# Zeros of the expert table written during attention, input sums by DMA, and a changed order of boxes, casts and router steps

## The chip, the cores and the metric

The kernel runs on one core of a Trainium2 chip. The metric is the device time of one execution in microseconds (us). Engines: PE (TensorE, matmuls), DVE (VectorE), ACT (ScalarE), POOL (GpSimd) and SP (SyncE, which here only issues DMAs). Each engine runs its own instructions in the order in which the program issues them, and waits on semaphores for the others. DMAs are issued on the queues of SP, ACT and POOL.

## The reference

Three stages follow each other.

```python
# attention: B=4, H=8, S=576, D=64; heads 0-3 local (32), heads 4-7 strided (32)
scores = np.where(masks, scale * q @ k.T, -1e9); attn = softmax(scores); x = attn @ v
x = transpose(x).reshape(2304, 512)
# gated unit: d_ff = 1536
x = ((1 / (1 + np.exp(-(x @ w_gate)))) * (x @ w_val)) @ w_out
# routed experts: E = 8, F = 1024; only tokens with x @ w_skip > 0
e_idx = argmax(x @ w_gate2); gate_w = softmax(x @ w_gate2)[e_idx]
out = x;  out[do_compute] += gate_w * (relu(x @ w1[e]) @ w2[e])
```

Everything is float32.

## The kernel before

**Numbers.** Products in float32 are made of three matmuls (`mm3`, L592): each operand is split into a high part, cast to `fp32r` by ACT, and a low part, operand minus high, made by DVE. `xh`, `xl` are parts of the inputs, `wh`, `wl` of the weights.

**Attention (0 to 119 us).** 32 steps, each one batch and a pair of heads. A string of letters (`ORDERS` and its default, L874) says in which order a step issues its pieces: scores on PE, row maxima on DVE, exponentials on ACT, the reciprocal of sums on DVE (L308), the norm on POOL (L314), the transposing "flip" on PE (L323), the product with V on PE (L339), and from there a copy into `xf`, the transposed input of the next stage (L345, L351). `a`, `D` and `p` in the string take one job from the background queues of ACT, DVE and POOL. Three more steps drain the pipeline and hold pieces of the first block (`G`). `step_loads` (L819) adds DMAs and background jobs at fixed steps.

**Blocks (to about 396 us).** The tokens are cut into six units of 384, in three pairs p. A pair's products with a pair of weight chunks f are done by a scheme of seven products: the inputs B11, B21, B22 and sums T1 to T4 of the four quarters (`SUMS`: T1 = B12 − B11, T3 = B22 − B12, T2 = B22 − T1, T4 = B21 − T2), the weights A11, A12, A22 and sums S1 to S4. `combine` (L411) makes a job for a T, `operand` (L421) the jobs for its high and low. `stage_sums` (L517) makes the S, `split_w` (L526) the highs (L534) and lows (L537) of a weight block. `period` (L673) issues one block (f, p) interleaved with the end of the block before it: products (`mm`, L593 to L595), copies from PSUM on ACT (L625, L632, L636) and sums on DVE (L639, L655, L658, L666), then stores by DMA (L644). Its `freed` mark lets the next block's highs take the buffers. Weight bits are converted on DVE (L460, L464, L469, L489). "Boxes" `wof` hold two chunks of the out-weights and their sums (`out_weights`, L550), which are stored by DMA. `raws_left` is the list of raw weights in the order in which they are fetched.

**Stage 2 (396 to 552 us).** The product with w_out, 63 steps (`NSTEP`). `at(k, ...)` hangs extra work on a step. `load_x` and `load_w` fetch the stored sums; `turn_back` (L1073) multiplies with the identity and the router weights at once, and reads the result as rows (L1088, ACT) and router sums (L1089, DVE). `pick` chooses the expert, `place` (L1130) computes slots and scatters the rows by indirect DMA (L1147) to the table `xs` in DRAM. `init_xs` (L1189) writes zeros into the table before that, 13 DMAs on SP at steps 9 to 15.

**Experts.** For each of eight experts: fetch rows of `xs`, transpose (`prep`), hidden rows (`hidden`, L1478: matmuls L1488, sums L1501, the operation `h` L1508), outputs (`output_steps`, L1565). `split_e` (L1165) splits the expert's weights, high on ACT (L1168), low on DVE or POOL (L1169). The last unit's router (unit 5) is run inside expert 0's first rows, at the end of the function.

The lines on which the low parts and the sums rest:

```python
nc.vector.tensor_tensor(xl[p, nm][:, part, :], source(p, nm)[:, part, :], h.bitcast(F32), op=ALU.subtract)   # L433
e.tensor_tensor(source(p, nm)[:, part, :], x, y, op=ALU.subtract)                                           # L417
eng = nc.gpsimd if e and (i % 2 if e == 1 else i < 4) else nc.vector                                        # split_e
```

Of the kernel before, what the change touches and what calls it, by code (L numbers as in the profile page):

```python
# [14 lines left out]
I32 = mybir.dt.int32  # L15
# [8 lines left out]
def kernel(  # L24
# [73 lines left out]
    xs = dram.tile([NE * SLOTS, TW], F32, name="xs")  # L98
    vcm = dram.tile([B, S, 4 * D], F32, name="vcm")
# [231 lines left out]

    def apply_v(it, s, pT):
# [77 lines left out]

    def combine(p, nm, eng, parts, cost):  # L411

        e = nc.gpsimd if eng == "P" else nc.vector
# [7 lines left out]
    def operand(p, nm, parts, hc, lc):  # L421

        for part in parts:
            def high(part=part):
# [4 lines left out]
                nc.scalar.copy(xh[p, nm][:, part, :], source(p, nm)[:, part, :])  # L429

            def low(part=part):
                h = xh[p, nm][:, part, :]
                nc.vector.tensor_tensor(  # L433
                    xl[p, nm][:, part, :], source(p, nm)[:, part, :], h.bitcast(F32), op=ALU.subtract)

            j = Job("A", hc, high, [sum_job[p, nm]] if nm[0] == "T" else [])
            x_jobs.setdefault((p, nm), []).append(Job("D", lc, low, [j]))
# [79 lines left out]
    def stage_sums(f):  # L517
        for i, x, y, op in ((4, 0, 1, ALU.add), (5, 4, 2, ALU.subtract), (6, 2, 0, ALU.subtract), (7, 3, 5, ALU.subtract)):
            def fn(i=i, x=x, y=y, op=op):
                nc.vector.tensor_tensor(stage(f, i), stage(f, x), stage(f, y), op=op)  # L520
# [152 lines left out]
    def period(k, prev):  # L673
# [144 lines left out]

    def step_loads(t):  # L819
        clock[0] += 1  # L820
        b, j = divmod(t, 8)
# [53 lines left out]
    for t in range(NS + 3):  # L875
        for c in ORDERS.get(t, "eSfEmIFnaNDTMRpDAaL"):
# [17 lines left out]
    raws_left += [(NC - 1, "o")]  # L894
# [105 lines left out]
    for f, p in BL:  # L1000
# [72 lines left out]
    def turn_back(u, a):  # L1073
# [7 lines left out]
        for m in range(nb):  # L1081
# [83 lines left out]
    def split_e(e, i, raw):  # L1165
        eng = nc.gpsimd if e and (i % 2 if e == 1 else i < 4) else nc.vector
# [20 lines left out]
    zero = []  # L1187

    def init_xs():  # L1189
        zero = late.tile([128, TW], F32, tag="row", bufs=8, name="zero")  # L1190
        nc.gpsimd.memset(zero, 0.0)
        nc.gpsimd.memset(zero[:, TW - 1:TW].bitcast(I32), 1 << 16)
        for i in range(NE * SLOTS // 128):
            nc.sync.dma_start(xs[128 * i:128 * i + 128, :], zero)
            if i % 2:
                yield

# [147 lines left out]
    gx = init_xs()  # L1345
    for k in range(9, 16):
        at(k, gx)
    for p in range(NP):
# [12 lines left out]
        if last:  # L1361
            for k, n in ((15, 1), (16, 2)):
                at(b + k, ta[1], n)
# [446 lines left out]
```

## Time and profile before

| | us |
|---|---|
| median of three runs (lowest, highest) | 745.8 (745.15, 747.28) |
| the profiled execution, own time | 746.98 |
| its span in the profile | 745.3 |
| PE busy | 706.2 |
| DVE busy | 561.6 |
| ACT busy | 452.0 |
| POOL busy | 258.9 |

The mean granted TensorE clock is 0.99 of full speed. The page gives busy time by engine, slices of the span, the chain of waits that ended last, and the costliest groups of instructions. Timelines give for each instruction its start, its duration, the engine and the line, what it writes and reads, and in brackets how long the engine had stood idle before it and what ended that. The waits view sums such idle times by the operation that waited and the one that released it. Windows give the busy time of each engine in a stretch, the granted clock and the share of the DMA engines.

### The profile page before, as it was taken

Reading aid. Unit: us, or ns where it says so; the run is one execution under the profiler, and the core shown is the slowest. Engines: PE = TensorE matmul, PEld = TensorE weight load, DVE = VectorE, ACT = ScalarE, POOL = GpSimd, SP = SyncE. Lnnn points to the kernel's source line nnn. Section 1 sums busy time; section 2 is a strip of 40 time slices with the busy share of each in tenths; the row PEclk is TensorE's granted clock in tenths of the full one; section 3 lists DMA queues with packets and bytes.
Section 4 is the critical chain, followed back from the end, with each engine's and each line's share of the span. In section 5 each row is a group of like instructions: output and inputs, shape, how many; then the busy total and the mean of one; then the engine's idle time right before and its main releaser. Section 6 shows DMA issues by size and latency. Waiting matters only on the chain. (4 is left out here: it accounts for less than half of the span.)

```text
span 745.3 us, 14548 instructions
## 1 busy us (share of the span) xinstructions
PE 706.2 (95%) x4785; PEld 660.1 (89%) x4785; DVE 561.6 (75%) x1246; ACT 452.0 (61%) x1206; POOL 258.9 (35%) x289
## 2 busy tenths in 40 slices
PE   8999988999999999999998989999999999999992
PEld 5766666999999999999888989999988899999991
DVE  3799997989988888888876766677766666666650
ACT  5888986855555555555454855566644766676730
POOL 6577876021040211204033000402324644566611
PEclk9999999999999999999999999999999999999997
DMA  9999610296898888979599996879845687776710
GB/s 199 234 209 220 149 42 30 107 258 187 275 222 256 209 222 228 224 263 202 177 274 335 368 332 180 257 244 303 289 144 186 203 259 246 225 250 223 225 39 14
DMA packets 136857, 158.57 MB, mean 213 GB/s; under 512 B 60510, under 2 KB 105822, under 8 KB 136776
## 3 DMA queue, kind: packets, MB, share of 16 engines
q1 hardware_dynamic: 122072, 134.51, 58.6%
q0 software_dynamic: 11936, 19.66, 12.9%
q10 hardware_dynamic: 2768, 3.41, 1.3%
q8 instruction: 40, 0.66, 0.4%
q14 instruction: 41, 0.34, 0.1%
HBM read 103.49 MB, written 59.65 MB: 219 GB/s over the span
## 5 line engine op out<-in xcount | busy, mean ns | idle before, releaser
L644 POOL DMA_DIRECT2D gT<-sC x36 | 31.9, 1030 | 171.2 <-DVE sC L658 163.9
L301 ACT ACTIVATE sm<-psX,mx 96x128 f32<-96x128 f32 (+2 forms) x176 | 61.8, 375 | 10.1 <-DVE mx L295 7.9
L314 POOL TENSOR_TENSOR sm<-sm,rs 96x384 f32<-96x384 f32 (+2 forms) x64 | 55.5, 885 | 31.6 <-DVE rs L308 18.8
L985 ACT CAST xt<-xt 128x768 fp32r<-128x768 f32 (+1 forms) x74 | 53.9, 742 | 20.5 <-DMA xt<-gB 11.0
L993 DVE TENSOR_TENSOR xt<-xt 128x768 fp32r<-128x768 f32 (+1 forms) x74 | 60.6, 833 | 7.3 <-ACT xt L985 7.2
L639 DVE TENSOR_TENSOR u<-psD,u 128x384 f32<-128x384 f32 x70 | 38.7, 552 | 18.6 <-PE psD L595 18.3
L593 PE MATMUL psD<-xhT,wh 128*128 128x384 f32 x140 | 47.3, 338 | 1.6 <-DVE u L639 1.6
L595 PE MATMUL psA<-xhB,wl 128*128 128x384 f32 x140 | 47.0, 336 | 1.3 <-DVE wl L537 1.3
L595 PE MATMUL psD<-xhT,wl 128*128 128x384 f32 x140 | 47.1, 337 | 0.3 <-DVE wl L537 0.3
L594 PE MATMUL psD<-xlT,wh 128*128 128x384 f32 x140 | 47.0, 336 | 0.0
L594 PE MATMUL psA<-xlB,wh 128*128 128x384 f32 x140 | 46.8, 334 | 0.0
L593 PE MATMUL psA<-xhB,wh 128*128 128x384 f32 x140 | 46.8, 334 | 0.0
L595 PE MATMUL psB<-xhT,wl 128*128 128x384 f32 x140 | 46.8, 334 | 0.0
L593 PE MATMUL psB<-xhT,wh 128*128 128x384 f32 x140 | 46.8, 334 | 0.0
L594 PE MATMUL psB<-xlT,wh 128*128 128x384 f32 x140 | 46.8, 334 | 0.0
L632 ACT COPY psC<-psB 128x384 f32<-128x384 f32 x35 | 16.3, 465 | 43.4 <-PE psB L595 43.4
L1575 POOL DMA_INDIRECT out_dram<-xg x16 | 16.1, 1006 | 73.8 <-DVE xg L1574 65.4
L625 ACT COPY u<-psB 128x384 f32<-128x384 f32 x70 | 33.8, 483 | 11.3 <-PE psB L595 11.1
L1120 POOL COPY row<-lm_all 128x8 f32<-128x8 f32 x18 | 7.9, 478 | 90.1 <-DVE lm_all L1116 90.1
L301 ACT ACTIVATION_READ_ACCUMULATOR sm<-psX,mx 96x1 f32 (+2 forms) x176 | 38.3, 218 | 0.0
L594 PE MATMUL psB<-xt,wtS 128*128 128x384 f32 x108 | 36.3, 336 | 0.9 <-DVE xt L993 0.9
L593 PE MATMUL psB<-xt,wtS 128*128 128x384 f32 x108 | 36.9, 342 | 0.0
(798 smaller groups left out, 2546.7 us busy)
## 6 DMA issues: line engine op xcount, KB each, us to landing
w1r<-in_moe_w_dram SPq DMA_DIRECT2D x28, 512.0 KB
w2r<-in_moe_w_dram SPq DMA_DIRECT2D x28, 512.0 KB
xt<-gT SPq DMA_DIRECT2D x30, 384.0 KB
gT<-u SPq DMA_DIRECT2D x54, 192.0 KB
xt<-gB SPq DMA_DIRECT2D x22, 384.0 KB
gT<-sC POOLq DMA_DIRECT2D x36, 192.0 KB, 6.1
gB<-sA SPq DMA_DIRECT2D x33, 192.0 KB
wg<-in_moe_w_gate_dram SPq DMA_DIRECT2D x12, 512.0 KB
```

What stands on the lines that cost most here:

```text
L301: nc.scalar.activation(sm[:n, w, 0:c], src[:, w, :], AF.Exp, bias=mx[:n, w:w + 1], accum_out=sums[:n, h, w:w + 1])
L314: nc.gpsimd.tensor_tensor(x, x, rs[:n, h, 0:m].rearrange("p (w o) -> p w o", o=1).to_broadcast([n, m, c]), op=ALU.mult)
L593: nc.tensor.matmul(ps, lhsT=whi, rhs=xhi, start=start, stop=False, skip_group_check=skip)
L594: nc.tensor.matmul(ps, lhsT=whi, rhs=xlo, start=False, stop=False, skip_group_check=skip)
L595: nc.tensor.matmul(ps, lhsT=wlo, rhs=xhi, start=False, stop=stop, skip_group_check=skip)
L625: nc.scalar.copy(self.tm[nm], self.ps["B"])
L632: nc.scalar.copy(ps, self.ps[src])
L639: nc.vector.tensor_tensor(self.tm[nm], self.ps["D"], self.tm[nm], op=ALU.add)
L644: nc.gpsimd.dma_start(dst, t, accum_op=ALU.add)
L985: nc.scalar.copy(h.bitcast(F32R), l)
L993: nc.vector.tensor_tensor(l.bitcast(F32R), l, h, op=ALU.subtract)
L1575: ins = nc.gpsimd.indirect_dma_start(out=out[:, :], out_offset=bass.IndirectOffsetOnAxis(ap=xg[t][:n, TW - 1:TW].bitcast(I32), axis=0), in ...
```

## The change

**Zeros.** `init_xs` now runs inside attention. At step 18 three memsets on POOL fill two tiles, two DMAs write them into a DRAM tile `empty` of 128 rows, and at steps 21 to 33 one DMA a step on SP copies it into 128 rows of `xs`.

**Input sums.** Signs are turned so that T1 and the other sums of pair 1, and T1 of pair 2, become additions: `put_x` multiplies by −1 where it copied, and B11's high and low turn it back. A sum is then a copy of one operand by a DMA on SP (`begin_sum`) and a DMA on POOL's queue that adds the other (`accum_op`). The lows of pair 1's B21, T3 and T2 go to POOL. One more background job of POOL is taken in each step after 24.

**Weights and boxes.** `period` asks for block 2's casts and lows (`need(w_jobs[2][0])`) before the sums of the last block of chunk 0. Box 9 is converted before the weights of block 11, and its raw weights are fetched before theirs. The sums S change sign order, with operations of one kind for another.

**Router and tail.** `turn_back` reads the router sums before the rows. Unit 4's and 5's router steps and the transpose of expert 0's rows sit at other steps, unit 5's chain in the tail is written in another order, with the gate's exponential behind it. The odd lows of expert 1 (`split_e`) go from POOL to DVE.

```diff
+    def put_x(dst, src, turned):
+        if turned:
+            nc.vector.tensor_scalar(dst, src, -1.0, None, op0=ALU.mult)
+        else:
+            nc.vector.tensor_copy(dst, src)
...
+    def begin_sum(p, nm):
+        nc.sync.dma_start(source(p, nm), source(p, SUMS[nm][0]))
+
     def combine(p, nm, eng, parts, cost):
...
-                e.tensor_tensor(source(p, nm)[:, part, :], x, y, op=ALU.subtract)
+                t = source(p, nm)[:, part, :]
+                if p == 0 or eng == "D":
+                    (nc.vector if eng == "D" else nc.gpsimd).tensor_tensor(t, x, y, op=ALU.add)
+                else:
+                    nc.gpsimd.dma_start(t, y, accum_op=ALU.add)
...
+                if turned:
+                    nc.vector.scalar_tensor_tensor(l, in0=x, scalar=-1.0, in1=h, op0=ALU.mult, op1=ALU.subtract)
+                else:
+                    (nc.gpsimd if eng == "P" else nc.vector).tensor_tensor(l, x, h, op=ALU.subtract)
...
             if prev.p == NP - 1:
                 freed[prev.f].done = clock[0]
+                if prev.f == 0:
+                    need(w_jobs[2][0])
             prev.store("sC", "u4", 1)
...
+    def init_xs(t):
+        n = NE * SLOTS // RB
+        if t == 18:
+            z, last = temp("zeros"), temp("empty")[:, 0:TW - UT]
+            nc.gpsimd.memset(z, 0.0)
+            nc.gpsimd.memset(last, 0.0)
+            nc.gpsimd.memset(last[:, TW - UT - 1:TW - UT].bitcast(I32), 1 << 16)
+            nc.sync.dma_start(empty[:, 0:UT], z)
+            nc.sync.dma_start(empty[:, UT:TW], last)
+        if 21 <= t < 21 + n:
+            nc.sync.dma_start(xs[RB * (t - 21):RB * (t - 20), :], empty[:, :])
...
-        if t == 22:
-            combine(1, "T1", "P", HALVES, 1.0)
+        if t == 23:
+            begin_sum(1, "T1")
             operand(1, "B11", HALVES, 0.5, 0.5)
-        if t == 26:
+        if t == 25:
+            combine(1, "T1", "P", WHOLE, 0.7)
+        if t == 27:
             for nm in ("T3", "T2", "T4"):
-                combine(1, nm, "P", HALVES, 1.0)
-            for nm in ("B21", "T3", "T2"):
-                operand(1, nm, HALVES, 0.5, 0.5)
-        if t == 30:
-            combine(2, "T1", "P", HALVES, 1.0)
+                begin_sum(1, nm)
+            operand(1, "B21", HALVES, 0.5, 0.9, "P")
+        if t == 29:
+            for nm in ("T3", "T2"):
+                combine(1, nm, "P", WHOLE, 0.7)
+        if t == 31:
+            combine(1, "T4", "P", WHOLE, 0.7)
+            begin_sum(2, "T1")
+        if t == 32:
+            for nm in ("T3", "T2"):
+                operand(1, nm, HALVES, 0.5, 0.9, "P")
+        if t == 33:
+            combine(2, "T1", "P", WHOLE, 0.7)
...
-        for c in ORDERS.get(t, "eSfEmIFnaNDTMRpDAaL"):
+        for c in ORDERS.get(t, "eSfEmIFnaNDTMRpDAaL" + "p" * (t > 24)):
...
-    raws_left += [(NC - 1, "o")]
+    raws_left[-4:] = [raws_left[i] for i in (-2, -4, -3, -1)] + [(NC - 1, "o")]
...
+            if f == NC - 2:
+                out_weights(outs_of[f][0], more_raw)
             if f + 1 < NC:
                 weights(f + 1, more_raw)
-            for i in outs_of[f]:
+            for i in outs_of[f][f == NC - 2:]:
                 out_weights(i, more_raw)
...
-        eng = nc.gpsimd if e and (i % 2 if e == 1 else i < 4) else nc.vector
+        eng = nc.gpsimd if e > 1 and i < 4 else nc.vector
...
-    at(NSTEP - 2, do(lambda: pp.extend(prep(0, head["xg"], PARTS[:1], tag="Y"))))
+    at(NSTEP - 3, do(lambda: pp.extend(prep(0, head["xg"], PARTS[:1], tag="Y", gates=False))))
...
-            for k, n in ((15, 1), (16, 2)):
-                at(b + k, ta[1], n)
+            at(b + 16, ta[1], 3)
...
-            for k in range(18, 21):
-                at(b + k, tb[1])
-            for k in (19, 20):
-                at(b + k, g, 3)
+            at(b + 19, tb[1], 3)
+            at(b + 20, g, 6)
...
-    evict = hidden(1, w, pp, hts, 0, HEAD)
     run(turn_back(NU - 1, 0))
-    evict()
+    evicts = [hidden(1, w, pp, hts, 0, HEAD)]
     run(pick(NU - 1))
-    hide(2, 3)
+    evicts.pop()()
+    evicts = [hidden(2, w, pp, hts, 0, HEAD)]
+    run(place(NU - 1, rank_sums(rst[NU - 1][1])))
+    evicts.pop()()
+    hide(3)
+    gate(xg, pp, 0, HEAD)
     sums = output_steps(0, HEAD, w, hts, xg, pp, settle)
     run(sums, 2)
-    run(place(NU - 1, rank_sums(rst[NU - 1][1])))
```

How the change moves instructions at three places follows. A row is a line of the kernel, an operation, what it writes and reads with a number for each tile, and the shape.

POOL at the end of attention before, from the second half of norm 28 to the last sum (`sm` are the softmax rows, `xT21` is T2 of pair 1, `xT41` its T4, `xT12` T1 of pair 2):

```order
L314 TENSOR_TENSOR sm_2088<-sm_2088,rs_2125 126x2x126
L417 TENSOR_TENSOR xT21_2154<-x31_1497,xT11_1897 128x384
L314 TENSOR_TENSOR sm_2122<-sm_2122,rs_2190 108x3x108
L314 TENSOR_TENSOR sm_2146<-sm_2146,rs_2190 108x3x108
L417 TENSOR_TENSOR xT21_2154<-x31_1497,xT11_1897 128x384
L314 TENSOR_TENSOR sm_2187<-sm_2187,rs_2238 126x2x126
L314 TENSOR_TENSOR sm_2201<-sm_2201,rs_2238 126x2x126
L417 TENSOR_TENSOR xT41_2256<-x21_963,xT21_2154 128x384
L314 TENSOR_TENSOR sm_2235<-sm_2235,rs_2290 108x3x108
L314 TENSOR_TENSOR sm_2253<-sm_2253,rs_2290 108x3x108
L417 TENSOR_TENSOR xT41_2256<-x21_963,xT21_2154 128x384
L417 TENSOR_TENSOR xT12_2364<-x50_2029,x40_1498 128x384 x2
```

Now, from the second low of B21 on (`xlB211`, `xlT31` are lows of pair 1, `xT31` its T3):

```order
L454 TENSOR_TENSOR xlB211_2095<-x21_964,xhB211_2094 128x384
L431 DMA xT31_2054<-x30_1504 128x768
L315 TENSOR_TENSOR sm_2142<-sm_2142,rs_2207 108x3x108
L315 TENSOR_TENSOR sm_2163<-sm_2163,rs_2207 108x3x108
L431 DMA xT21_2056<-xT11_1796 128x768
L315 TENSOR_TENSOR sm_2204<-sm_2204,rs_2255 126x2x126
L315 TENSOR_TENSOR sm_2218<-sm_2218,rs_2255 126x2x126
L431 DMA xT41_2058<-xT21_2056 128x768
L315 TENSOR_TENSOR sm_2252<-sm_2252,rs_2304 108x3x108
L315 TENSOR_TENSOR sm_2266<-sm_2266,rs_2304 108x3x108
L454 TENSOR_TENSOR xlT31_2320<-xT31_2054,xhT31_2319 128x384 x2
L431 DMA xT12_2277<-x40_1506 128x768
```

The half sums between the norms are gone; three DMAs stand there instead, T2's ahead of norm 30 and T4's, which reads T2, ahead of norm 31, with two lows behind it.

DVE at the end of block (0, 2) before (`u4_02`, `sC_02` and so on are that block's sums, `wl32` and `wl42` the lows of weight block 2):

```order
L639 TENSOR_TENSOR u4_02_2737<-psD_2664,u4_02_2737 128x384
L520 TENSOR_TENSOR stage21_2661<-stage20_2660,stage21_2661 128x256
L655 SCALAR_TENSOR_TENSOR sC_02_2768<-sC_02_2768,u4_02_2737 128x384
L639 TENSOR_TENSOR u2_02_2700<-psD_2664,u2_02_2700 128x384
L658 TENSOR_TENSOR sA_02_2713<-sA_02_2713,u2_02_2700 128x384
L666 TENSOR_TENSOR u2_02_2700<-sA_02_2713,sC_02_2768 128x384
L537 TENSOR_TENSOR wl32_2789<-stage20_2660,wh32_2788 128x768
L537 TENSOR_TENSOR wl42_2806<-stage21_2661,wh42_2805 128x1024
```

Now:

```order
L664 TENSOR_TENSOR u4_02_2758<-psD_2685,u4_02_2758 128x384
L541 SCALAR_TENSOR_TENSOR stage21_2682<-stage21_2682,stage20_2681 128x256
L562 TENSOR_TENSOR wl32_2806<-stage20_2681,wh32_2805 128x768
L680 SCALAR_TENSOR_TENSOR sC_02_2789<-sC_02_2789,u4_02_2758 128x384
L664 TENSOR_TENSOR u2_02_2721<-psD_2685,u2_02_2721 128x384
L683 TENSOR_TENSOR sA_02_2734<-sA_02_2734,u2_02_2721 128x384
L691 TENSOR_TENSOR u2_02_2721<-sA_02_2734,sC_02_2789 128x384
L562 TENSOR_TENSOR wl42_2814<-stage21_2682,wh42_2813 128x1024
```

The first low has moved ahead of four sums, the second has stayed behind them.

POOL behind unit 5's scatter before (`we11l` to `we15l` are lows of expert 1, `out_0_dram<-xg00` the store of expert 0's first rows):

```order
L1147 DMA xs_69<-row50_6997,si_7229 1664x521
L1147 DMA xs_69<-row51_6998,si_7229 1664x521
L1147 DMA xs_69<-row52_6999,si_7229 1664x521
L1169 TENSOR_TENSOR we11l_7313<-w1r11_7103,we11h_7312 128x1024
L1575 DMA out_0_dram<-xg00_6856 2304x512
L1169 TENSOR_TENSOR we13l_7428<-w1r13_7310,we13h_7427 128x1024
L1169 TENSOR_TENSOR we15l_7534<-w2r15_7425,we15h_7533 128x1024
```

Now:

```order
L1200 DMA xs_69<-row50_7028,si_7204 1664x521
L1200 DMA xs_69<-row51_7029,si_7204 1664x521
L1200 DMA xs_69<-row52_7030,si_7204 1664x521
L1611 DMA out_0_dram<-xg00_6861 2304x512
L1611 DMA out_0_dram<-xg01_6862 2304x512
L1222 TENSOR_TENSOR we20l_7609<-w1r20_7575,we20h_7608 128x1024
```

Expert 1's lows have left POOL; the next low there is one of expert 2.

## Rows read from the trace of the kernel before

**Rows 1.** The page, part 1: busy us, share of the span, instructions.

```profile
PE 706.2 (95%) x4785; PEld 660.1 (89%) x4785; DVE 561.6 (75%) x1246; ACT 452.0 (61%) x1206; POOL 258.9 (35%) x289
```

**Rows 2.** Waits of PE, 100 to 120 us: total us, times, longest.

```profile
PE psY L323 <- POOL sm L314: 2.0, 7, 0.4
```

**Rows 3.** Timeline of POOL, 115 to 125 us: start, duration, idle before.

```profile
115.75 1.53 POOL L314 TENSOR_TENSOR sm<-sm,rs 108x324 f32<-108x324 f32 x2 [0.56 <-DVE rs L308]
...
122.48 1.53 POOL L314 TENSOR_TENSOR sm<-sm,rs 108x324 f32<-108x324 f32 x2 [0.49 <-ACT psX L632]
```

**Rows 4.** Line 417, POOL: duration ns min/median/max, starts.

```profile
L417 POOL TENSOR_TENSOR xT<-x,x x10: 994/1242/1452, 62.4 to 126.3; 128x384 f32<-128x384 f32 x10
```

**Rows 5.** Line 433, one form on DVE: duration ns min/median/max.

```profile
L433 DVE TENSOR_TENSOR xlB<-x,xhB x14: 512/782/1501, 87.2 to 149.4; 128x384 fp32r<-128x384 f32 x10, 128x768 fp32r<-128x768 f32 x4
```

**Rows 6.** Line 214, DMAs of V on POOL: ns on POOL, us to landing.

```profile
L214 POOL DMA_DIRECT2D vcm<-in_v_dram x16: 643/655/852, 6.7 to 92.5; - x16
...
DMA to landing us min/median/max: 2.6/4.3/5.2
```

**Rows 7.** Line 644, block stores on POOL, 192 KB: us to landing, min/median/max.

```profile
DMA to landing us min/median/max: 3.8/6.2/9.8
```

**Rows 8.** Windows, 110 to 120 us: busy of each engine, clock, DMA share, GB/s.

```profile
110.00:120.00 10.00, 8.79 (x94) 6.24 (x93) 9.43 (x26) 8.59 (x40) 7.79 (x9) 1.00 0.01 2
```

**Rows 9.** Timelines around the lows of blocks 1 and 2: PE, ACT, DVE.

```profile
139.46 0.44 PE L595 MATMUL psD<-xhT,wl 128*128 128x384 f32 x1 [0.28 <-DVE wl L537]
...
166.29 1.78 ACT L534 CAST wh<-stage 128x768 fp32r<-128x768 f32 x2 [0.38 <-PE psD L594]
...
166.46 0.56 DVE L639 TENSOR_TENSOR u<-psD,u 128x384 f32<-128x384 f32 x1 [2.04 <-PE psD L595]
...
168.12 2.08 DVE L537 TENSOR_TENSOR wl<-stage,wh 128x768 fp32r<-128x768 f32 x2
...
169.13 0.44 PE L595 MATMUL psA<-xhB,wl 128*128 128x384 f32 x1 [1.30 <-DVE wl L537]
```

**Rows 10.** Timelines around box 10's conversion: DVE, PE.

```profile
365.69 0.43 DVE L460 TENSOR_SCALAR wof<-wo 128x512 int32<-128x512 int32 x1 [2.02 <-DMA wS<-wof]
...
368.44 0.44 PE L593 MATMUL psD<-xhT,wh 128*128 128x384 f32 x1 [1.64 <-DVE u L639]
```

**Rows 11.** The stall at the end of the blocks: PE's timeline, and the window.

```profile
393.16 0.69 PE L593 MATMUL psC<-xhB,wh 128*128 128x384 f32 x1 [3.63 <-ACT psC L632]
...
392.00:396.00 4.00, 2.84 (x9) 2.84 (x10) 1.79 (x3) 1.90 (x4) 0.00 (x0) 0.64 1.09 306
```

**Rows 12.** Line 1194, the writes of zeros on SP: ns, first and last start.

```profile
L1194 SPq DMA_DIRECT2D xs<-zero x13: 319/320/621, 416.3 to 434.4; - x13
```

**Rows 13.** Windows of 4 us in stage 2.

```profile
436.00:440.00 4.00, 3.10 (x17) 2.59 (x16) 3.36 (x6) 2.01 (x4) 0.00 (x0) 1.00 1.08 321
440.00:444.00 4.00, 3.71 (x24) 3.25 (x22) 1.07 (x4) 2.69 (x6) 0.00 (x0) 1.00 1.01 382
444.00:448.00 4.00, 2.94 (x17) 2.57 (x17) 4.00 (x9) 2.59 (x6) 0.00 (x0) 1.00 0.43 156
```

**Rows 14.** Waits of PE, 520 to 560 us.

```profile
PE psY L1087 <- DVE s L1283: 1.3, 2, 1.1
PE psY L1232 <- DVE base_e L1063: 0.5, 1, 0.5
PE psY L1086 <- DVE lp L1089: 0.2, 1, 0.2
```

**Rows 15.** Waits of PE, 560 to 586 us; timelines of POOL and DVE.

```profile
PE psZ L1565 <- DVE h L1508: 1.5, 1, 1.5
PE psY L1488 <- DVE hs L1501: 0.8, 1, 0.8
...
565.91 2.65 POOL L1169 TENSOR_TENSOR we11l<-w1r,we11h 128x1024 fp32r<-128x1024 f32 x1 [0.31 <-issue]
...
566.25 2.46 DVE L1508 SCALAR_TENSOR_TENSOR h<-hs,h 128x128 fp32r<-128x128 f32 x1
```

More of the change, by code (lines that the diff above doesn't have):

```diff
@@ L98 @@
     xs = dram.tile([NE * SLOTS, TW], F32, name="xs")
+    empty = dram.tile([RB, TW], F32, name="empty")
     vcm = dram.tile([B, S, 4 * D], F32, name="vcm")
@@ L416, in fn, with operand @@
                 x, y = (source(p, z)[:, part, :] for z in SUMS[nm])
-                e.tensor_tensor(source(p, nm)[:, part, :], x, y, op=ALU.subtract)
+                t = source(p, nm)[:, part, :]
[3 more added lines that the diff above has]
+                    nc.gpsimd.dma_start(t, y, accum_op=ALU.add)
             before = [sum_job[p, z] for z in SUMS[nm] if z[0] == "T"]
             sum_job[p, nm] = Job(eng, cost, fn, before)
-    def operand(p, nm, parts, hc, lc):
+    def operand(p, nm, parts, hc, lc, eng="D"):
+        turned = nm == "B11"
         for part in parts:
@@ L428, in high @@
                     xl[p, nm] = part_x(f"xl{nm}{p}", l, F32R)
-                nc.scalar.copy(xh[p, nm][:, part, :], source(p, nm)[:, part, :])
+                if turned:
+                    nc.scalar.mul(xh[p, nm][:, part, :], source(p, nm)[:, part, :], -1.0)
+                else:
+                    nc.scalar.copy(xh[p, nm][:, part, :], source(p, nm)[:, part, :])
             def low(part=part):
-                h = xh[p, nm][:, part, :]
-                nc.vector.tensor_tensor(
-                    xl[p, nm][:, part, :], source(p, nm)[:, part, :], h.bitcast(F32), op=ALU.subtract)
+                h, x, l = xh[p, nm][:, part, :].bitcast(F32), source(p, nm)[:, part, :], xl[p, nm][:, part, :]
+                if turned:
+                    nc.vector.scalar_tensor_tensor(l, in0=x, scalar=-1.0, in1=h, op0=ALU.mult, op1=ALU.subtract)
+                else:
+                    (nc.gpsimd if eng == "P" else nc.vector).tensor_tensor(l, x, h, op=ALU.subtract)
             j = Job("A", hc, high, [sum_job[p, nm]] if nm[0] == "T" else [])
-            x_jobs.setdefault((p, nm), []).append(Job("D", lc, low, [j]))
+            x_jobs.setdefault((p, nm), []).append(Job(eng, lc, low, [j]))
     raw_of, stage_of, wh, wl, w_jobs, wo_jobs = {}, {}, {}, {}, {}, {}
@@ L517, in stage_sums, with fn @@
     def stage_sums(f):
-        for i, x, y, op in ((4, 0, 1, ALU.add), (5, 4, 2, ALU.subtract), (6, 2, 0, ALU.subtract), (7, 3, 5, ALU.subtract)):
-            def fn(i=i, x=x, y=y, op=op):
-                nc.vector.tensor_tensor(stage(f, i), stage(f, x), stage(f, y), op=op)
+        for i, x, y in ((4, 0, 1), (5, 2, 4), (6, 0, 2), (7, 5, 3)):
+            def fn(i=i, x=x, y=y):
+                if i == 7:
+                    nc.vector.scalar_tensor_tensor(
+                        stage(f, i), in0=stage(f, x), scalar=-1.0, in1=stage(f, y), op0=ALU.mult, op1=ALU.subtract)
+                else:
+                    nc.vector.tensor_tensor(
+                        stage(f, i), stage(f, x), stage(f, y), op=ALU.add if i == 4 else ALU.subtract)
             last = Job("D", 0.35, fn)
@@ L1091, in turn_back @@
             )
+            nc.scalar.copy(row[m][:, 256 * a:256 * a + 256].rearrange("p (c n) -> p c n", c=2), pr[:, :, 0:128])
             yield
@@ L1186 @@
     w_e0, pp = [], []
[L1187 to L1196, printed above, removed]
     PARTS = ((0, HEAD), (HEAD, SLOTS))
@@ L1344 @@
             at(j + g, do(lambda g=g, nm=nm: w_halves(nm, g)))
-    gx = init_xs()
-    for k in range(9, 16):
-        at(k, gx)
     for p in range(NP):
```

7 lines of the change are left out of this document (3 added, 4 removed).

## The prediction

> **What bounds the kernel now.** The page's first part comes first: PE is busy for 706.2 us, 95% of the 745.3 us span [rows 1], so a change can only pay where PE stands still, or where it makes PE stand still. I therefore read PE's waits stretch by stretch, then the row of the engine named as releaser, then what that engine waited for. The same groups serve each part below. A measurement of this kernel tells about 0.3%, 2.2 us, from no change.
>
> In the last 20 us of full attention steps PE waits 2.0 us in seven places for POOL's norms [rows 2]. But POOL itself stood idle before those norms until DVE's reciprocal came [rows 3]: there the chain runs through DVE, not through POOL's sums. In the first blocks PE waits for a weight block's lows [rows 9], and late in the blocks for a sum that stands behind a box conversion [rows 10]. Up to 444 us the DMA engines are full, and PE falls short of 4.00 us in three stretches of 4 us [rows 13]. Between 520 and 586 us PE waits six times for DVE, together 4.3 us [rows 14, 15].
>
> **A. Pair 1's sums, lows and attention's drain: +0.5 us.** POOL loses ten half sums at a median of 1.242 [rows 4], 12.4 us. It gains five DMA issues: the nearest row, DMAs of V on the same queue, has 0.643 to 0.852 each [rows 6], so 3.2 to 4.3 us. It also gains six lows of the half sums' shape at about the same 1.24, so 7.4 us. POOL's load hardly falls, and it moves late: one low and three of the DMAs now stand among norms 28 to 31. DVE loses the six lows: at 0.512, 0.782 or 1.501 each [rows 5], between 3.1 and 9.0 us, by the median 4.7. SP's five copies are issued two or more steps ahead of their sums, and SP has thirteen zero copies beside them: nothing, as long as those steps cover the landing; without that cover the sum's DMA holds POOL as below. The three memsets on POOL at step 18 are at most a half sum each, and POOL stood idle before its norms [rows 3]: nothing, else 3.7 us of POOL once. The turned signs change operations into ones of the same size: nothing.
>
> What of this reaches PE: a gain of at most the 2.0 us that it waits for norms [rows 2], through an earlier DVE. Against it stands a new wait: the DMA for T4 reads T2, so it waits on POOL until T2's accumulation has landed, and norm 31 is queued behind it. Norm 29 ended at 117.3 before [rows 3]; a low and a DMA issue are now ahead of it, so T2's DMA is issued near 118. Landing is bounded by 2.6 (a DMA of V) and 9.8 us (a block store) [rows 6, 7]. I take 5, between the smallest and the store's median of 6.2, since their share of busy time is 0.01 there [rows 8]. Norm 31 then starts near 123.9 instead of 122.48 [rows 3], about when PE comes to it. Later, T2's lows on POOL and DVE's sums between two SBUF tensors meet: that a low took 1.501 instead of 0.512 beside POOL's norms [rows 5] shows the price of such a meeting. The wait of 0.28 for a weight low [rows 9] grows to about 1.3. I take −0.5 for the earlier DVE and +1.0 for that: +0.5, with ends −2 and +2.
>
> **B. Casts of block 2 ahead of the sums: +1.1 us.** ACT's high cast for block 2 waits for PE to leave the old one, as now: the pair of casts begins at 166.29 and the first, 768 of 1792 columns of 1.78, ends near 167.1 [rows 9]. DVE's first low then runs 167.1 to 168.0 (768 of 1792 columns of 2.08 are 0.89). So the first matmul that waited, until 169.13 [rows 9], comes 1.0 earlier. But four sums of 128x384, at 0.56 each [rows 9], now stand between the two lows: the second low begins near 170.2 and ends, after 1.19, near 171.4. It ended at 170.2 before (168.12 + 2.08). The matmul that reads it comes six matmuls after the first, at 170.3, so PE wins 1.0 and then waits 2.2: net +1.1. The ends are −1.3, the whole wait gone, if DVE slips the sums in while ACT still casts, and +1.3.
>
> **C. Box 9 converted before block 11's weights: −1.6 us.** DVE stands 2.02 us before box 10's conversion until stores of the boxes before, from the same buffers, have landed, and PE then waits 1.64 for the sum queued behind [rows 10]. With 23 DVE operations between the two conversions the stores have landed. What is late next is block 11's two lows, behind the eight operations of box 9 that moved ahead of them: by the order and the durations of these forms they come near 362.5 and 363.6, and PE wants them near 366 and 367. Ends −1.7 and −0.8.
>
> **D. The stall before 393.16: nothing.** PE waits 3.63 us for ACT, which waits for loads, and the matmul after it takes 0.69 [rows 11]. The change touches neither the loads nor the order there. Ends −1.5 and +1.
>
> **E. The zeros leave stage 2: −2.25 us.** Thirteen writes of 260.5 KB, 3.4 MB, were issued from 416.3 to 434.4 [rows 12]. With DMA at 321 to 382 GB/s [rows 13] they took about 9 us of it. DMA falls from 1.01 to 0.43 behind 444, so loads there caught up late. PE's shortfall in the three stretches is 0.90 + 0.29 + 1.06 = 2.25 [rows 13]; loads that come 9 us of transfer earlier end it. Ends −2.6 and −0.5. In attention their cover is idle DMA engines [rows 8]; without it they would take the same 9 us of transfer from loads of a later block.
>
> **F. Router, unit 5 and expert 1's lows: −3.6 us.** PE's waits of 1.3, 0.5 and 0.2 belong to unit 4's and 5's router steps and to the gate's sums behind them [rows 14], and those of 1.5 and 0.8 to hidden rows [rows 15]. The last two have one cause: DVE's operation on `h` took 2.46 while POOL's low ran from 565.91 for 2.65 [rows 15]; the second wait follows a like pair. These lows go to DVE, four at 1.2 each, by the 2.08 for 1792 columns of such lows [rows 9]; DVE is free for that, and if it weren't each would cost PE up to 1.2. So 4.3 go, less 0.7 for three router turns in one step that share two banks: each of two may wait as long as the 0.2 to 0.5 of [rows 14]. Reading the sums before the rows only swaps who waits for whom: nothing. Unit 5's scatter is issued about 5 us earlier; nobody waited for it. Ends −4.2 and −1.5.
>
> **Sum:** 0.5 + 1.1 − 1.6 + 0 − 2.25 − 3.6 = −5.85. The profiled execution took 746.98 for a span of 745.3; it would become 741.1. It is 1.2 above the median of the runs, 745.8, so the median becomes 740.0.
>
> **Rivals.**
> 1. More comes through. In B DVE fits its sums in while ACT casts (−1.3 instead of +1.1), and in A the whole 2.0 of [rows 2] goes (−2 instead of +0.5): 4.9 better, 735.1. For it: POOL waited for DVE [rows 3]. Against: the order of DVE's program in B. Chance 0.2.
> 2. Gains come back as other waits. The stages are DMA- or chain-bound behind the waits that go: E keeps 0.5, F 1.5, C 0.8, beside A and B: 0.5 + 1.1 − 0.8 − 0.5 − 1.5 = −1.2, 744.6. For it: a DMA share over 1.0 right up to 444 [rows 13], which the next loads could fill at once. Against: it falls to 0.43 there. Chance 0.15.
> 3. Slower: POOL blocked by its accumulating DMAs. One moves 384 KB and reads its target too; with the store's median of 6.2 for 192 KB [rows 7], twice that is 12.4 for the landing. T4's DMA then leaves near 130.4, norm 31 starts at 131.3 instead of 123.9, and PE loses 7.4. After the wait of 3.63 PE's granted clock was 0.64 over 4 us, below the upper of its two levels, 2.4 GHz [rows 11]: 1.4 us of work lost; 740.0 + 7.4 + 1.4 = 748.8. It decides from a landing of some 12 us on; below 5 it costs nothing. Against: the DMA engines are nearly idle then. Chance 0.1.
>
> The rows of V's DMAs show 0.643 to 0.852 on POOL while DVE was busy [rows 6]: no sign of an issue that is held by DVE. The Trainium skill, "SBUF — State Buffer", section "SBUF: two separate sides", warns of just that: a DMA from POOL's queue needs descriptors that POOL cannot write while a DVE operation in its two-port mode holds the shared port pair, and it gives 3100 ns in place of 620. By that rule the three issues ahead of norms 29 to 31 would cost 3 × 2.48 = 7.4 us, an estimate from that page, and the time would be 747.4; by the row it is nothing, and the row decides.
>
> **How the numbers follow.** My forecast has 0.55 and its own range is 737 to 743.5; rival 1 has 0.2, rival 2 0.15, rival 3 0.1. The likeliest gives 740.0. From 735.5 to 745.0 leaves out rival 3 and the lower half of rival 1. Faster by over 0.3% (below 743.6) are the forecast and rival 1: 0.75; within 0.3% rival 2: 0.15; slower 0.1.
>
> **What would show it.** A: POOL's wait before T4's DMA, and norm 31's start; a landing over 6 us is a step wrong. B: PE's wait at the second low, about 2 us, in place of 1.30 at the first. C: no 2.02 before box 10. D: 3.6 still there. E: 4.00 of 4.00 in PE's three stretches. F: DVE's `h` back under 0.4 and the six waits at most 0.7 together. If A and B together exceed +4, or E's shortfall stays, the forecast is wrong.

## The result and the profile after

The changed kernel is slower: the median is 752.2 us (747.54 to 755.99) against 745.8 (744.59 to 747.77), a ratio of 1.0069 with a 95% interval of 1.0052 to 1.0086. The ratio and its interval, here and below, are of the executions in the chip's fast state, and are not the quotient of the two medians, which is 1.0086 here. Forecast were 740.0 and a gain. The profiled execution took 749.25 us, 3 less than the median, with a span of 747.5 against 745.3, 2.3 longer; its last matmul of the experts starts at 736.62 instead of 731.30, 5.3 us later. The other 3.1 are a shorter stretch behind that matmul, for which no cause was found (see the last section).

The rest of the comparison goes by such marks. The two profiles line up as follows (starts in us, from PE's timelines; the lows of block 4 from DVE's). The first mark is one and the same matmul in every kernel, the 156th of L593 to L595 in the trace; the expectations below call it the 160th.

| mark | before | after | later by |
|---|---|---|---|
| 156th matmul of the weight blocks | 152.57 | 155.99 | 3.4 |
| lows of block 4 | 203.28 | 207.84 | 4.6 |
| first matmul of stage 2 | 397.24 | 401.49 | 4.3 |
| last matmul of the experts | 731.30 | 736.62 | 5.3 |

So the change lost 3.4 us by the end of attention, another 1.1 at block 2, and in the second half, where E and F had 5.85 us of gains, it lost one more.

Waits of PE in the profile after, from 100 to 120, 120 to 140, 160 to 180, 380 to 400, 400 to 420, 520 to 560 and 560 to 590 us (total us, times, longest):

```profile
PE psY L324 <- POOL sm L315: 2.5, 4, 1.7
...
PE psY L324 <- POOL sm L315: 2.4, 2, 2.2
...
PE psD L620 <- DVE wl L562: 1.6, 1, 1.6
PE psA L620 <- DVE wl L562: 0.4, 1, 0.4
...
PE psC L618 <- ACT psC L657: 4.7, 1, 4.7
...
PE psA L618 <- ACT psB L1498: 4.1, 1, 4.1
...
PE psY L1139 <- ACT row L1144: 0.5, 2, 0.3
PE psB L619 <- DVE xt L1044: 0.5, 1, 0.5
...
PE psY L1139 <- DVE hs L1537: 0.7, 1, 0.7
PE psZ L1591 <- ACT h L1540: 0.4, 1, 0.4
PE psY L1524 <- DVE cp L1189: 0.4, 1, 0.4
```

The rows of before are [rows 2, 9, 11, 14, 15]. Gone are the wait of 1.64 before box 10 [rows 10], the shortfall of [rows 13], and part of the tail's waits: 4.3 became 2.5. New are 1.7 and 2.2 for POOL's norms, 4.1 for a copy on ACT near 412, and the stall at the blocks' end has grown from 3.63 to 4.7.

POOL's timeline at attention's end (start, duration, idle before), with one row of SP's:

```profile
100.92 0.97 POOL L431 DMA_DIRECT2D xT<-x  x1 [2.75 <-DVE mx L296]
101.58 1.97 POOL L315 TENSOR_TENSOR sm<-sm,rs 96x384 f32<-96x384 f32 x2
...
118.69 1.12 POOL L431 DMA_DIRECT2D xT<-xT  x1
...
118.84 1.83 SPq L857 DMA_DIRECT2D xs<-empty  x2
...
127.14 0.88 POOL L431 DMA_DIRECT2D xT<-xT  x1 [5.65 <-DMA xT<-xT]
127.73 1.74 POOL L315 TENSOR_TENSOR sm<-sm,rs 108x324 f32<-108x324 f32 x2
```

T1's sum waited 2.75 us before it could start, and norm 25 behind it. T2's sum was issued at 118.69; T4's, which reads it, started at 127.14, so that T2's took about 8 us to land. The last two copies of zeros were issued right beside it, at 118.84. Norm 31 began at 127.73, where [rows 3] have 122.48.

Windows of the profile after (busy time of PE, PEld, DVE, ACT, POOL; granted clock, DMA share, GB/s):

```profile
100.00:104.00 4.00, 1.98 (x21) 1.37 (x20) 2.40 (x7) 2.09 (x13) 2.63 (x3) 1.00 0.89 241
104.00:108.00 4.00, 4.00 (x31) 2.95 (x30) 2.53 (x8) 3.28 (x16) 2.05 (x2) 0.56 1.02 262
108.00:112.00 4.00, 4.00 (x34) 3.13 (x35) 3.37 (x9) 2.73 (x11) 2.15 (x3) 0.59 1.07 404
412.00:416.00 4.00, 3.98 (x15) 3.98 (x16) 2.20 (x3) 2.40 (x4) 0.00 (x0) 0.62 1.04 410
436.00:440.00 4.00, 4.00 (x25) 4.00 (x25) 2.69 (x5) 3.81 (x7) 0.00 (x0) 1.00 0.87 238
440.00:444.00 4.00, 4.00 (x25) 4.00 (x25) 3.99 (x7) 3.10 (x6) 0.00 (x0) 1.00 0.70 192
444.00:448.00 4.00, 4.00 (x26) 4.00 (x25) 3.26 (x7) 1.11 (x2) 0.00 (x0) 1.00 0.63 184
```

From 100 to 112 us the DMA engines, at 0.10 before, are now at 0.89 to 1.07, and after the stretch in which PE was busy for only 1.98 us of 4.00 its clock is granted at 0.56 and 0.59 for 8 us. That is near the lower of its two levels, 1.2 of 2.4 GHz. In stage 2 PE is at 4.00 in all three windows of [rows 13].

The new stall, seen from SP, ACT and PE (SP's row is a group of three loads; the second row is from SP's waits):

```profile
386.60 15.35 SPq L1029 DMA_DIRECT2D wtA<-wA  x3
...
SPq L1029 <- PE psD L620: 13.0, 1, 13.0
...
408.64 0.83 ACT L1036 CAST xt<-xt 128x768 fp32r<-128x768 f32 x1 [8.93 <-DMA xt<-gB]
...
412.02 0.69 PE L618 MATMUL psA<-xt,wtA 128*128 128x384 f32 x1 [4.09 <-ACT psB L1498]
```

SP spends 15.35 us on three loads of out-weight sums, 13.0 of them in one wait for the last product of the weight blocks (psD). Every load behind it on SP's queue is late: ACT waits 8.93 us for a token block, PE 4.09 us for ACT's copy, and behind that wait its clock is granted at 0.62 from 412 to 416.

DVE's operation on `h`, after:

```profile
562.71 0.28 DVE L1544 SCALAR_TENSOR_TENSOR h<-hs,h 128x128 fp32r<-128x128 f32 x1
```

`h` takes 0.28 where it took 2.46 [rows 15], as forecast.

**Where the 13.0 us come from.** The buffers of the built programs, that is the addresses that their tiles get, show it. Stage 2 loads the weight sums into buffers that the blocks' operands used before. Before, A12's second part (`wtA121`, the first of these loads on SP) followed T3's high of pair 1, and S2's third part (`wtS22`, on POOL's queue) followed T4's high of pair 2 (`xhT42`). T4's high of pair 2 is read by the very last product of the blocks. The changed sums allocate their tiles in another order, and now `wtA121` follows `xhT42`. Its load cannot start until the blocks are over, and the loads behind it on SP's queue start after it. The order of SP's loads there is the same in both kernels, and both carry a wait for PE on that load: only the buffer, and so the matmul waited for, differs.

### The profile page after: what moved, and what is told of

Its sections match the earlier page's. It is cut to its first block, busy times and chain, and to the rows that moved or that the text cites. A ratio compares the mean times of both kernels' runs of the same rounds, so it can differ in the third digit from the quotient of the medians.

```text
span 747.5 us, 14576 instructions
## 1 busy us (share of the span) xinstructions
PE 709.4 (95%) x4785; PEld 663.6 (89%) x4785; DVE 554.7 (74%) x1244; ACT 452.6 (61%) x1206; POOL 245.6 (33%) x287
## 5 line engine op out<-in xcount | busy, mean ns | idle before, releaser
L324 PE MATMUL psY<-ident,sm 96*128 96x96 f32 (+2 forms) x176 | 28.0, 274 | 10.4 <-POOL sm L315 9.6
```

Source lines behind the costliest of these rows:

```text
L324: nc.tensor.transpose(pp[:, w, :], sm[:n, w, 0:c], ident[:n, :n])
```

## The experiments

Theory 1: the sums by DMA cost it all, through that buffer and through late landings on POOL. Theory 2: the zeros in attention. Theory 3: stage 2 lacks DMA time. Each run also has the kernel before on the same chip; ratios are against it. The next table has all of them.

| run | parts | median us | before | ratio (95%) |
|---|---|---|---|---|
| e1 | the change, buffers traded | 742.94 | 745.28 | 0.997 (0.9946 to 0.9993) |
| e2 | the change without sums by DMA | 741.31 | 745.28 | 0.9945 (0.9925 to 0.9966) |
| e3 | sums by DMA alone | 750.59 | 745.28 | 1.0064 (1.0045 to 1.0084) |
| e4 | zeros in attention alone | 743.68 | 745.28 | 0.9979 (0.9966 to 0.9992) |
| e5 | e1 without early casts | 739.67 | 745.16 | 0.993 (0.9908 to 0.9953) |
| e6 | e1, zeros in the weight blocks | 736.94 | 745.16 | 0.9883 (0.986 to 0.9906) |
| e7 | router, unit 5 and lows alone | 741.2 | 745.16 | 0.9952 (0.9934 to 0.997) |
| e8 | e6 without early casts | 735.06 | 745.16 | 0.986 (0.9839 to 0.9881) |
| e9 | before, buffers traded | 753.97 | 745.53 | 1.011 (1.0072 to 1.0149) |
| e10 | early casts alone | 745.85 | 745.53 | 1.0012 (0.9982 to 1.0041) |
| e11 | box order alone | 743.11 | 745.53 | 0.9944 (0.9916 to 0.9972) |
| e12 | e8, zeros in stage 2 as before | 734.55 | 745.53 | 0.9843 (0.9806 to 0.9881) |

**e1, buffers traded.** One line moves, in the changed kernel:

```diff
-    load_w("S2", 2, eng=nc.gpsimd)
-    for nm, g in (("A12", 1), ("A12", 2), ("S2", 0)):
+    load_w("A12", 1)
+    load_w("S2", 2, eng=nc.gpsimd)
+    for nm, g in (("A12", 2), ("S2", 0)):
         load_w(nm, g)
```

Buffers are handed out in the order in which they are first written, so A12's second part now gets the one that S2's third had.

> The changed kernel with one line moved: the load of A12's second part is written ahead of the load of S2's third, so that the two trade buffers. Theory 1 (the input sums by DMA moved the high part of T4 of pair 2, read by the last product of the blocks, into the buffer of the first late weight load, and SP's queue stands 13.0 us before that load): the 13.0 us wait of SP is gone, PE's wait of 4.1 us near 412 is gone with its stretch at a lower clock, and the time falls by 4 to 7 us, to 745 to 748. Theory 2 (the loss comes from attention: zeros copied while the DMA engines are full) or theory 3 (a general shortage of DMA in stage 2): SP's queue waits for DMAs anyway, PE's wait of 4.1 us stays within 1 us, the time stays at 751 to 753.

It fell from 752.2 to 742.94, more than expected. SP's three loads, POOL's issue of T2's sum with its landing, T4's sum, and PE's waits from 520 to 590:

```profile
388.82 2.58 SPq L1029 DMA_DIRECT2D wtA<-wA  x3
...
115.95 1.11 POOL L431 DMA_DIRECT2D xT<-xT  x1
...
DMA to landing us min/median/max: 9.5/9.5/9.5
...
125.75 0.87 POOL L431 DMA_DIRECT2D xT<-xT  x1 [7.01 <-DMA xT<-xT]
...
PE psY L1139 <- DVE hs L1538: 0.7, 1, 0.7
PE psY L1139 <- ACT row L1144: 0.6, 2, 0.3
```

The three loads take 2.58 us instead of 15.35, and PE has no wait left from 400 to 420, so theory 3 falls: the order of the loads' buffers was enough. From the first matmul of stage 2 to the last of the experts it is 327.17 us (402.85 to 730.02) instead of 335.13: 8.0 us from the buffer. T2's sum still lands late, 9.5 us from its issue, with T4's start 0.3 behind; that loss is still there, and norm 31 now holds PE up for 3.6 us. In the tail PE waits 1.3 us, not the 2.5 of the changed kernel.

**e2, no sums by DMA.** All the change's lines for `put_x`, `begin_sum`, `combine`, `operand`, `stage_sums` and the steps' jobs are taken back.

> The change without its input sums by DMA (the sums and lows of pair 1 back on POOL and DVE, signs as before), all other parts kept. Theory 1 (the sums by DMA cost it all, by POOL's waits for landings in attention's end and by the buffer): the gains of the boxes, the zeros and the tail show, 738 to 742; PE's waits for POOL between 100 and 140 us are at most 3 us together and no wait of 13 us stands in SP's queue. Theory 2 (zeros in attention load the DMA engines and delay q, k and v): 746 to 750, PE loses time around 100 us all the same and its clock falls there.

741.31. Waits of PE from 120 to 140 and 160 to 180 us:

```profile
PE psY L324 <- POOL sm L315: 0.3, 1, 0.3
...
PE psD L596 <- DVE wl L538: 1.6, 1, 1.6
PE psA L596 <- DVE wl L538: 0.4, 1, 0.4
```

No wait for a landing is left at attention's end although the zeros are copied there, so the zeros alone don't do it: theory 2 falls (e4 has them quite alone). The loss at block 2 is unchanged.

**e3, sums by DMA alone.**

> The kernel before with the input sums by DMA alone (with their signs, the lows on POOL, the extra POOL jobs). Theory 1: slower by 5 to 12 us, 751 to 758, with POOL waiting 4 us or more for a landing before T4's DMA, and SP's queue waiting 10 us or more for the last product. Theory 2 (the zero copies are what fills the DMA engines in attention): without them the copies land within 3 us, POOL waits under 3 us, and the time is 744 to 749.

750.59. POOL's issue of T2's sum with its landing, T4's sum, PE's wait from 400 to 420, SP's wait from 370 to 412:

```profile
115.04 1.11 POOL L430 DMA_DIRECT2D xT<-xT  x1
...
DMA to landing us min/median/max: 5.4/5.4/5.4
...
120.71 0.87 POOL L430 DMA_DIRECT2D xT<-xT  x1 [2.88 <-PE psY L346]
...
PE psA L617 <- ACT psB L1496: 5.9, 1, 5.9
...
SPq L1012 <- PE psD L619: 12.2, 1, 12.2
```

The buffer's stall is there in full (12.2 and 5.9 us). But attention is shorter: the 156th matmul of the blocks starts at 149.53, 3.0 us earlier than before. T4's sum starts 5.7 us after T2's issue; the row names PE for its wait, but here too it starts 0.3 us behind T2's landing. So half of theory 1 was wrong here: I had expected POOL to hold PE up without the zeros too.

**e4, zeros alone.**

> The kernel before with the zeros written in attention alone. Theory 1: stage 2 gains what it did in the changed kernel, PE at 4.00 of 4.00 from 436 to 448, attention unchanged within 1 us: 742 to 745. Theory 2: attention loses 3 us or more to late loads of q, k or v around 100 us, more than stage 2 gains: 746 to 750.

743.68. Windows in attention and in stage 2:

```profile
96.00:100.00 4.00, 3.52 (x39) 2.48 (x38) 3.90 (x10) 4.00 (x20) 3.02 (x3) 1.00 1.10 295
100.00:104.00 4.00, 3.40 (x38) 2.39 (x37) 3.91 (x10) 3.36 (x17) 3.01 (x3) 1.00 0.90 268
...
444.00:448.00 4.00, 4.00 (x28) 4.00 (x27) 2.13 (x6) 2.34 (x6) 0.00 (x0) 1.00 0.41 123
```

The zeros fill the DMA engines to 1.10 and PE's work goes on: the mark stands at 152.00, 0.6 earlier than before. In the profiles of before and of the runs that leave attention alone (e7, e9, e10, e11) this mark lies from 151.71 to 152.62, so 0.6 is nothing.

**e5, without the early casts.** From e1 the two lines with `need(w_jobs[2][0])` go.

> The first experiment's kernel (buffers traded) without the early casts of block 2. Theory 1 (the early casts put four sums between the two lows and cost 1.1 us, as worked out; in the first experiment's profile PE's clock fell behind that wait too, 1.6 us more): PE waits 1.3 us at the first low instead of 2.0 at both, the stretch from the 160th matmul of the blocks to the lows of block 4 shrinks from 51.85 (53.4 with the fall of the clock) to 50.7 us, and the time falls by 1 to 3 us to 740 to 742. Rival (later slack takes the wait up): no change of the time beyond 0.5 us.

739.67, 3.3 below e1, slightly more than the 1 to 3 expected. From the 156th matmul to block 4's lows it is 50.69 us (156.95 to 207.64), as before (50.71); e1 had 53.41.

**e6, zeros in the weight blocks.** From e1:

```diff
-        if 21 <= t < 21 + n:
-            nc.sync.dma_start(xs[RB * (t - 21):RB * (t - 20), :], empty[:, :])
...
         k = Block(f, p)
+        i = 3 * f + p - 12
+        if 0 <= i < NE * SLOTS // RB:
+            nc.sync.dma_start(xs[RB * i:RB * (i + 1), :], empty[:, :])
```

> The first experiment's kernel with the thirteen copies of zeros issued one by one ahead of blocks 12 to 24 of the weight blocks, not in attention. Theory 1 (zeros and sums by DMA hurt only together: alone each made attention shorter, the sums by 3.0 us and the zeros by 0.6, together they made it 3.4 to 4.7 us longer, since the sums' copies and adds land behind the zeros): the landing of T2's sum falls under 6 us, attention's end comes 6 us or more earlier than in the first experiment, and the time is 735 to 739. Rival (the zeros' transfer costs the same wherever it stands, since the blocks use 0.8 to 0.97 of the DMA engines): 741 to 745, with new waits of PE in the blocks.

736.94, 6.0 us below e1's median. T2's and T4's sums on POOL:

```profile
116.17 1.11 POOL L431 DMA_DIRECT2D xT<-xT  x1
...
122.73 0.87 POOL L431 DMA_DIRECT2D xT<-xT  x1 [3.77 <-DVE x L336]
```

T4's sum starts 6.6 us after T2's issue, at 122.73 instead of 125.75, and the mark stands at 151.54 instead of 157.25. The landing was expected under 6 us and took 6.3, and the mark was expected 6 us earlier and is 5.7; PE waits for norms no more than 0.5 us from 120 to 140. PE's waits view has none in the blocks from 180 to 380.

**e7, the tail alone.**

> The kernel before with the router's and unit 5's order and expert 1's lows on DVE alone. Theory 1: PE's waits between 520 and 590 us fall from 4.3 to about 1.5 us; 742 to 744, nothing else moves. Rival (the tail's gain came from other parts, an earlier stage 2): PE's waits there stay above 3 us and the time at 745 to 746.

741.2, better than expected. PE's waits from 520 to 590 us fell from 4.3 to 1.8 (1.5 expected), and stage 2 gained too, which was not expected. Its windows, with the zeros still written there:

```profile
436.00:440.00 4.00, 4.00 (x27) 4.00 (x26) 3.89 (x7) 2.62 (x5) 0.00 (x0) 1.00 1.05 382
440.00:444.00 4.00, 4.00 (x28) 4.00 (x26) 3.19 (x7) 3.32 (x8) 0.00 (x0) 1.00 0.74 266
444.00:448.00 4.00, 4.00 (x27) 4.00 (x27) 3.10 (x7) 2.67 (x6) 0.00 (x0) 1.00 0.33 98
```

PE is at 4.00 in each, where before it was at 3.10, 3.71 and 2.94 [rows 13]. From stage 2's first matmul to the experts' last it is 327.93 us (397.14 to 725.07) instead of 334.06.

**e8, all that gained.** e6 without the early casts.

> All parts of the change that gained, and none that lost: buffers traded, zeros in the weight blocks, no early casts of block 2. Theory 1: the sum of its parts against the kernel before, sums -3.0, boxes -1.6, zeros -2.25, tail -3.6 and less for waits that overlap: 735 to 738, and 1 us below the run with early casts. Rival (parts share their waits): 738 to 742.

735.06, as theory 1 had it, 1.9 below e6. But the number came out by luck: theory 1 added up some 10.5 us of PE's waits, and the last matmul of the experts starts only 7.9 earlier than before (723.44). The other 3.1 of the 11.0 by which the span is shorter stand behind that matmul, where theory 1 has nothing.

**e9, the converse.** The line of e1 moved in the kernel before, and nothing else. There the same line gives A12's second part the buffer of `xhT42`.

> The converse of the first experiment: the kernel before, nothing of the change in it, with the same one line moved, so that the load of A12's second part gets the buffer of T4's high of pair 2. Theory 1 (the buffer alone makes the stall): SP's queue waits 10 us or more for the last product of the blocks, PE waits 4 to 6 us near 405, and the time rises by 5 to 8 us to 750 to 753, with attention and blocks as before. Rival (the stall needs the changed kernel's late start or its loads): at most 1 us slower.

753.97. SP's wait and PE's:

```profile
SPq L978 <- PE psD L595: 10.9, 1, 10.9
...
PE psA L593 <- ACT psB L1463: 4.5, 1, 4.5
```

The time is at the upper end of what was expected, 750 to 753, and a little over it. Attention and blocks are as before; from stage 2's first matmul to the last it is 340.23 us (395.96 to 736.19), 6.2 more than before. With e1 this settles the buffer: it makes the stall in a kernel with nothing else of the change, and without it the changed kernel has no stall.

**e10, early casts alone.**

> The kernel before with the early casts of block 2 alone. Theory 1: PE waits 0.4 at the first low and 1.6 at the second instead of 1.3, the stretch from the 160th matmul of the blocks to the lows of block 4 grows from 50.7 to 51.8 us, the time by 1 us, to 746 to 747, near the bound of what the runs can tell. Rival (a gain, as the first low comes earlier): 744 to 745.

745.85 with an interval around no change: the time alone tells neither. The trace does. PE at the two lows, and DVE at the first:

```profile
167.43 0.44 PE L595 MATMUL psA<-xhB,wl 128*128 128x384 f32 x1 [0.35 <-DVE wl L537]
...
170.68 0.44 PE L595 MATMUL psD<-xhT,wl 128*128 128x384 f32 x1 [1.64 <-DVE wl L537]
...
166.41 0.96 DVE L537 TENSOR_TENSOR wl<-stage,wh 128x768 fp32r<-128x768 f32 x1 [3.58 <-ACT wh L534]
```

PE waits 0.35 and 1.64 instead of 1.30 once; the stretch to block 4's lows is 51.86 us (151.83 to 203.69) instead of 50.71.

**e11, box order alone.**

> The kernel before with box 9 converted ahead of block 11's weights alone. Theory 1: the wait of DVE before box 10 and PE's wait of 1.6 us near 368 are gone, 743.5 to 744.5. Rival (the stall of 3.6 us at the blocks' end, which waits for loads, takes it up): PE waits 5 us there and the time stays at 745 to 746.

743.11. The wait before box 10 is gone, and the wait at the blocks' end is now

```profile
PE psC L593 <- ACT psC L632: 4.7, 1, 4.7
```

instead of 3.63. Of the 1.6 us 1.1 come back there, as the rival had it, and yet the time is at the lower end of theory 1's. What is gained appears in stage 2, where PE waits 0.2 us from 420 to 460 instead of 2.2. These are the two longest of the four waits there before:

```profile
PE psB L594 <- DVE xt L993: 0.9, 1, 0.9
PE psY L1087 <- DVE sl L1257: 0.8, 1, 0.8
```

**e12, zeros back in stage 2.** e8 with the zeros written as before the change.

> The best kernel so far with the zeros back in stage 2, where they stood before the change. Theory 1 (zeros and router order share one wait: with the order of the router alone PE was at 4.00 of 4.00 from 436 to 448 though the zeros were still there): within 1.5 us of the best, 734.5 to 737. Rival (the zeros' transfer costs stage 2 its own 2 us): 737 to 739.

734.55, the fastest of all together with e8 (735.06), 1.6% below the kernel before: with the rest of the change in place, it makes no difference that these runs can tell whether the zeros are written in the weight blocks or in stage 2. Of its gain, too, 2.9 us stand behind the last matmul.

## Why the prediction was wrong

**Missed: the buffer.** This and A's landing are the steps that failed. The prediction has no term for it. It followed each moved instruction and each queue, but not which buffer a tile gets when the sums' tiles are made in another order. It costs 8.0 us in the changed kernel's profile (e1) and 6.2 in the kernel before's (e9), and 9.3 and 8.4 us in the medians (8.8 for the first if each median is taken against the kernel before beside it). That alone turns the gain into a loss. Of what the prediction says, D's step, "The change touches neither the loads nor the order there", comes nearest and failed: the order of the loads is the same, and what the first late load waits for is not.

**A: wrong step, in the landing and its cover.** The prediction took a landing of 5 us "since their share of busy time is 0.01 there", and costed the zeros' copies at nothing since "their cover is idle DMA engines". It used the same idle engines for both edits. The copies fill them (1.02 and 1.07 in the profile after), and the sums' copies and adds land late beside them. T2's issue to T4's start is 8.4 us in the profile after, 9.8 in e1 and 8.4 in e5, where zeros and sums stand together; 5.7 in e3, 6.6 in e6 and e8, where they don't. The landing itself took 9.5 in e1 and 8.1 in e5 against 5.4 in e3, 5.8 in e12 and 6.3 in e6 and e8, and T4's sum starts 0.3 behind it in all six. The zeros go by SP's queue and T2's sum by POOL's, so an order within one queue does not explain that landing. The block mark moves by +3.4 (after), +4.7 (e1) and +4.4 (e5) against −3.0 (e3), −1.0 (e6) and −1.9 (e8). The mechanism of rival 3, T4's sum held until T2's has landed and norm 31 behind it, is what happened, though the price came out otherwise: PE lost not 7.4 us behind norm 31 but 2.2 there, and 1.7 behind T1's sum with 8 us at 0.56 to 0.59 of its clock. In e1 it was 3.6 and 1.2 with the clock at 1.00. Rival 3 had the direction, but most of the loss is the buffer's, which it doesn't have.

Part A by itself measured −3.0 in e3 and −1.0 to −2.8 in e6, e8 and e12, where +0.5 was forecast with ends of −2 and +2. The wait of 1.0 for T2's lows did not show. The waits for norms from 100 to 140 us, 2.3 before, were 1.2 in e3 and 2.4 in e6, so an earlier DVE explains the gain only in part; where the rest comes from was not tried. (The median of 0.782 for DVE's lows [rows 5] mixes two shapes.)

An issue on POOL took 0.87 to 1.21 us, not 0.64 to 0.85; the blocks' stores, with a mean of 1.03, were the nearer row. The Trainium skill, "SBUF — State Buffer", section "SBUF: two separate sides", gives some 3100 ns in place of 620 for a DMA of POOL's queue beside a copy of DVE's; no issue here comes near that, and whether DVE ran in the mode meant there no run shows. What POOL waited for ahead of T4's sum was T2's landing. Ahead of T1's the row names DVE, and in e1 and e5 the sum starts 0.6 us behind the landing of SP's copy for it.

**B: right.** +1.15 measured (e10), +1.1 forecast, with the mechanism as worked out: waits of 0.35 and 1.64 for 1.30, where 0.3 and 2.2 were worked out. In e1's profile PE's clock fell to 0.83 from 170 to 180 behind that wait, and the same stretch was 2.7 longer.

**C: right in its place, given back next door.** DVE's wait is gone; of the 1.6 us, 1.1 went into the stall at the blocks' end, since ACT waits there for loads (e11: 4.7 us in four waits, 4.3 before). D's "nothing" was +1.1 in the profile after.

**E: the gain came, but it wasn't the zeros' own.** PE is at 4.00 there. The prediction counted E's 2.25 as the price of the zeros' transfer. Moving them alone does end the shortfall (e4), but the zeros may stay (e7, e12) and PE is at 4.00 all the same, and the box order alone shrinks the waits to 0.2 (e11). One wait that any of three parts removes was put down to one of them. Part of it comes and goes by itself: in e10, which changes nothing there, PE waits 1.3 us from 420 to 460 instead of 2.2. The step in F that reading the sums before the rows "only swaps who waits for whom: nothing" is the one that I suspect, since it is the part of e7 that touches stage 2 there; it was not tried apart from the rest of e7.

**F: right, and somewhat smaller.** PE's waits in the tail are 2.5 us after, against the forecast 0.7, and 4.3 before; without the buffer's stall (e1) they are 1.3, so 3.0 of the forecast 3.6 came. `h` is at 0.28. E, F and the box order together took 6.9 us from the second half (335.13 − 8.0 against 334.06), where 5.85 were forecast for E and F. Only 5.2 of that are waits that the profile shows, 2.2 from 420 to 460 and 3.0 in the tail.

**The sum by the profile:** A with the zeros +3.4, B +1.15, C and D −1.6 + 1.1, a rest of +0.2; the buffer +8.0, E and F −6.9. That is +5.3 at the last matmul, as measured, with the rest and E and F taken as what is left over. It is the account of one execution, which was 3 us faster than the median.

## What to carry to other kernels

Before costing a change that makes tiles in another order, list for each of the first loads of the next stage whose buffer it gets and which instruction reads that last; a load on an ordered queue that inherits the last-read buffer stops everything behind it, and here a queue with nothing urgent behind was the place for it: on POOL's queue, in the kernel before and in e1, the load into that buffer held nothing up. When two edits are each costed at nothing because an engine is idle, cost them together: the cover can be spent once. And where several edits each remove the same wait, its price goes into the sum once, whichever of them is credited.

## What the runs showed of the hardware

- A DMA that adds onto 128x768 floats took 0.87 to 1.21 us on POOL to issue. T2's landed 5.4 to 6.3 us after its issue (e3, e12, e6, e8), and 8.1 to 9.5 us after it (e5, e1) where copies of zeros of 260.5 KB were issued beside it.
- PE's granted clock fell to 0.56 and 0.59 for 8 us after a stretch from 100 to 104 in which PE was busy for 1.98 us (after).
- From the start of the last matmul to the end of the span it is 13.7 to 14.1 us in before, e2, e4, e7, e9, e10 and e11, and 10.9 to 11.1 in the change, e1, e5, e6, e8 and e12; e3 has 12.0. It goes with the sums by DMA and is worth some 3 us of the span. The program's text behind the last matmul is the same in all of them; the cause stays open.
- The changed kernel's 15 executions spread over 8.5 us, those of before beside them over 3.2. That isn't a mark of the change: beside e9 to e12, the 23 executions of before spread over 9.4, with two at 752.9 and 753.0, and e10, with nothing of the sums, over 10.1. The cause stays open.
